# A block of small state matmuls moved by two visits in a fused Mamba-2 scan and feed-forward kernel

## The chip, the cores and the metric

The kernel runs on one core of a Trainium2 chip. Its time is the device time of one execution in microseconds. Three runs of the kernel before the change took 364.34, 364.67 and 365.81 us; their median, 364.67, is the time before. One more execution was profiled, and all durations below are from that one.

## The reference

Two blocks are computed one after the other, in float32. The first is a Mamba-2 scan over x of shape (4, 8, 768, 32) with 16 states per head. It can be evaluated in chunks. Within a chunk:

```
cum     = cumsum(log a)                      # along the chunk
y_intra = ((C B^T) * exp(cum_i - cum_j) * causal) x
y_inter = (C state) * exp(cum)               # what the state before gives
y       = y_intra + y_inter
state   = exp(sum log a) * state + sum_j exp(cum_end - cum_j) B_j x_j
```

Its output, reshaped to 3072 tokens of width 256, goes through the second block:

```
h = y @ w_in          # 256 -> 2048
g = h * cos(h)
out = g @ w_out       # 2048 -> 256
```

The feed-forward block holds nearly all the arithmetic.

## The kernel before

**Chunks and visits.** The kernel takes the 768 positions in chunks of 128 (`NC` = 6, numbered 0 to 5), and each chunk in two units of 64. A pass over chunk c runs the feed-forward block for that chunk in 16 visits (`NF` = 16). Visit n = 16 c + f computes 128 columns of h for one half of the chunk's tokens and the other, a bank of 128 × 512 numbers. While the pass over chunk c runs, the scan for chunk c + 1 is prepared piece by piece in its visits. Where the text says "visit 13" it means f = 13 of a pass.

**One visit.** On TensorE `first(n)` (L650) writes hp(n), the 128 × 512 slice of h, into a PSUM bank. Then a chain over two engines makes g: ScalarE rounds h / 2π to a whole number (`wind_k`, L667), VectorE subtracts it (`wind_w`, L673), ScalarE takes the cosine (`gate`, L682), VectorE multiplies it with hp (`gated`, L687). Last, GpSimd makes three sums of slices of the result, gd (`differ`, L712, L714 and L715), for a second product that takes seven multiplications in place of eight (`seven`, L836). TensorE's `second(n - 2)`, two visits later (`LAG` = 2), uses g and gd.

**Visits with seven products in the first matmul, too.** In visits 10 to 12 of the passes over chunks 2, 3 and 4, and in most of the pass over chunk 5 (`runs`, `sevens`), hp is also made with seven products (`first7`, L760 on TensorE). There VectorE and ScalarE add the parts together (L767 to L781) before hp is whole, and the rest of that visit's chain (`wind`, `gate`, `gated`) is issued one visit late, out of the list `late`.

**PSUM.** There are eight banks: two with the tag "h" for hp, two with "o" for the results of the second product, and two pairs with the tag "scan" (`pair`). A seven-product run takes both pairs at its start, one for a share of hp (`at_["hp"]`, its second, fifth, ... visit) and one for parts (`at_["m"]`). So in visits 10 to 14 of the passes over chunks 2, 3 and 4 the banks "h" go to visits 10, 12, 13 and 14 in turn, and visit 11 has a bank of a pair. In the pass over chunk 1 every visit uses the two banks "h" in turn.

**The scan of the next chunk.** In the pass over chunk c (1 to 4), for chunk c + 1: `inner2` (L603) makes C Bᵀ on TensorE; `weights` multiplies it with the decays on VectorE into m; `turn2` makes rT, C with its decay; `add_state` brings the states up to date on VectorE. Then come the two functions that make y in two pair buffers:

- `open2` (L611): 32 products of states with rT (L617), which open the sums of y, and, but for the last chunk, 32 products of x with weighed B through `sums` (L477), which make the sums for the coming states. In the trace each product is two records, so 64 + 64. They work on tiles of 32 × 64 and 64 × 32.
- `finish2` (L623): 64 products of x with m (L629), which close y, on tiles of 64 × 32. Its `take` then copies y on ScalarE into yT (L636), first for one half, then for the other, and the state sums into a new state tile (L489).

y, not complete before finish2, is the input of `first` from the next pass on.

**What sets the order.** It is written out by hand. Each engine executes its instructions in the order of the program and waits at semaphores for the others. Near the end of a pass the order on TensorE is: first(13), second(11), `open2`, first(14), second(12), first(15), `finish2`, second(13), first(0) of the next pass. On ScalarE in visit 15: `wind_k`, the first half of y (`take_y(0)`), `gate`, the second half with the states (`take_y(1)`). DMAs are issued from the queue of SyncE; none belongs to the two functions.

Of the kernel before, what the change touches and what calls it, by code (L numbers as in the profile page):

```python
# [25 lines left out]
def kernel(  # L26
# [18 lines left out]
    NC = S // P  # L45
    DM, DF = moe_w_in.shape
    KT = DM // P
    NF = DF // P
# [23 lines left out]
    def pair(name):  # L72

        return psum.tile([P, 2, 4 * P], FP32, tag="scan", bufs=2, name=name)
# [52 lines left out]
    def load(c, i):  # L127
        if c < NC:
            for s in range(2):
                (load_x if i in (1, 2) else load_b)(2 * c + i // 2, s)  # L130

    def group(q, s):
        return slice(32 * (q ^ s), 32 * (q ^ s) + 32)
# [477 lines left out]
    def open2(c):  # L611

        ys[c] = y = [pair("y") for _ in range(2)]
        for k, p, s, q in ((k, p, s, q) for k in range(2) for p in range(2) for s in range(2)
                           for q in range(4)):
            r, o_, i = group(q, s), W * (q % 2), (2 * k + p) * W
            PE.matmul(y[s][o_:o_ + W, q // 2, i:i + W], lhsT=after[2 * c + k - 1][r, s, p],  # L617
                      rhs=part[c, s][2][r, p, k * W:(k + 1) * W], start=(k == p == 0), stop=False,
                      tile_position=(r.start, o_), skip_group_check=True)
        for k in range(2 if c < NC - 1 else 0):  # L620
            sums(2 * c + 1 + k, [y[s][:, 0, (2 + k) * P:(3 + k) * P] for s in range(2)], group)

    def finish2(c):  # L623

        y = ys.pop(c)
        for k, p, t, s, q in ((k, p, t, s, q) for k in range(2) for p in range(2)
                              for t in range(2) for s in range(2) for q in range(4)):
            ss, i, h = slice(s * W, (s + 1) * W), (2 * k + p) * W, 4 * t + q
            PE.matmul(y[s][32 * q:32 * q + 32, t, i:i + W], lhsT=xrs[2 * c + k][ss, p, h],  # L629
                      rhs=m_of[2 * c + k][ss, p, h], start=False, stop=True,  # L630
                      tile_position=(s * W, 32 * q), skip_group_check=True)
        yT[c] = two.tile([P, 2, 2, 2 * P], FP32, tag="yT", name="yT")

        def take(k):
            for s in range(2):
                ACT.copy(out=yT[c][:, k, :, s * P:(s + 1) * P], in_=y[s][:, :, k * P:(k + 1) * P])  # L636
            if k and c < NC - 1:
                take_sums((2 * c + 1, 2 * c + 2), [y[s][:, 0, 2 * P:] for s in range(2)])
        return take
# [36 lines left out]
    def wind(n):  # L676
        wind_k(n)
        wind_w(n)

    def gate(n):  # L680
        cos = turns[n]
        ACT.activation(cos, cos, AF.Sin, bias=quarter, scale=TWO_PI)  # L682
# [421 lines left out]
    for n in range(AHEAD, NC * NF + LAG):  # L1104
        c, f = divmod(n, NF)
        if n < NC * NF:

            if c > 0 and f in (loads_of := (6, 7, 8, 9) if c == 1 else (0, 1, 2, 3)):
                load(c + 2, loads_of.index(f))
            if n in (NF - 4, NF - 3):  # L1110
                load_arow(n - NF + 8)
            if n == NF - 2:
                for k in (4, 5):
                    for s in range(2):
                        load_x(k, s)
            if n in (NF - 1, NF):
                load_along(2, (2 * (n == NF), 2 * (n == NF) + 1))
            for e, i in chunks_at(n, "along"):
                load_along(e + 1, (2 * i, 2 * i + 1))
            if n in sevens or n - 1 in sevens:  # L1120
                first_of_seven(n)
            else:
                first(n)
            if n not in sevens and n - 1 in sevens:
                wind(n - 1)
                gate(n - 1)
                gated(late.pop())
            closing = f == NF - 1 and 1 <= c < NC - 1
            take_y = finish2(c + 1) if closing else None
            if n not in sevens:  # L1130
                wind_k(n)
                wind_w(n)
            if closing:
                take_y(0)
            for e, s in chunks_at(n - 1, "turn"):
                turn2(e, s)
            for k in units_at(n, 2):
                turn_unit(k)
            if n + 1 in piece:
                rests_of.append(grade(*piece[n + 1], later=True))  # L1140
            if n not in sevens:
                gate(n)
            while len(rests_of) > (n == AHEAD):
                rest = rests_of.pop(0)
                if rest:
                    rest()
            joins = n in piece and piece[n] in held
            if joins:
                join(*piece[n])

            behind = [lambda at=at: decays2(*at) for at in decays_at(n)]
            behind += [lambda k=2 * c - 1 + i: add_state(k) for c, i in chunks_at(n, "state")]
            behind += [lambda c=c, b=2 * s + p: reaches(c, b) for c, s in chunks_at(n, "reach")
                       for p in range(2)]
            behind += [lambda at=at: turn_blocks(*at) for at in chunks_at(n, "turn")]
            behind += [lambda k=k, p=p: decays0(k, p) for k, at in unit_at.items()
                       for p in range(2) if at[0][p] == n]
            behind = [lambda k=2 * c + i, q=q: weights(k, q) for c, i in chunks_at(n, "weigh")
                      for q in range(2)] + behind
            behind = [lambda k=k: weights(k, 1) for k in units_at(n - 1, 3)] + behind  # L1160
            if not joins and behind:
                behind.pop(0)()
            if n + 1 in sevens or n in sevens:
                late.append(n)
            else:
                gated(n)
            if closing:
                take_y(1)
            if n == NF + 7:
                weigh0(5)  # L1170
            if add_s and (n == NF - 5 or units_at(n - 1, 4)):
                exchange = add_s()
                add_s = None
            if n == NF + 9:
                exchange()
            for do in behind:
                do()
            if n == runs[-1][0] - 2:
                for i in range(4):
                    differ_y(NC - 1, i, V)  # L1180
            if 2 <= c < NC - 1 and 4 <= f <= 7:
                differ_y(c, f - 4, G, slice(1, 2))
            if unsummed and (n in sevens or summed[0]):
                unsummed[0](range(summed[0], summed[0] + 1), G)
                summed[0] = (summed[0] + 1) % 4
                if summed[0] == 0:
                    unsummed.pop()
            elif n not in sevens and f not in ((10, 11, 12) if c == 1 else (10, 11)):
                for do in unsummed:
                    do()  # L1190
                unsummed.clear()
            for k, ((_, last_), *_) in unit_at.items():
                if last_ == n:
                    weigh0(k)
        for i, js in differ_at.get(n, ()):
            differ_w(i, js)
        for start, js in zip((2 * NF - 5, 3 * NF - 3, 4 * NF - 3),
                             (slice(2, 5), slice(0, 2), slice(5, NJ))):
            if start <= n < start + 4:
                differ_in(n - start, js)  # L1200
        if n == AHEAD + 1:
            second(AHEAD - LAG)
        if n >= LAG and n != AHEAD:
            second(n - LAG)
        for e, _ in chunks_at(n, "inner"):
            inner2(e)
        for k in units_at(n, 3):
            for t in range(2):
                inner(k, t)
            if k == 3:  # L1210
                at = [gs[k, s][:, 0, 2 * P:] for s in range(2)]
                sums(4, at, group)
                take_sums((4,), at)
            weights(k, 0)
        for k in units_at(n, 4):
            take_s, add_s = finish0(k)
            take_s()
        for k in units_at(n, 1):
            reach_unit(k)
        if f == NF - 3 and 1 <= c < NC - 1:  # L1220
            open2(c + 1)
        for at, e in block_loads.items():
            if at == n:
                loading = load_blocks(e)
            if at <= n < at + 12:
                next(loading)
# [30 lines left out]
```

## Time and profile before

| What | us |
|---|---|
| Runs: lowest, median, highest | 364.34, 364.67, 365.81 |
| Profiled execution, first to last instruction (the span) | 369.8 |
| TensorE, matmuls: busy | 359.4 (97%) |
| VectorE: busy | 270.8 (73%) |
| GpSimd: busy | 233.0 (63%) |
| ScalarE: busy | 182.3 (49%) |

The page gives the profiled execution's span and no other time of its own; it is 5.1 us longer than the median of the timed runs. The row of the granted clock shows full speed but for one slice of the forty, after a wait of 4.2 us on TensorE in the pass over chunk 1.

How to read it: a row of a timeline has the start, the time it took, the engine, the line of the kernel, the operation, what it writes from what it reads, the tile, and how many records are merged in the row. In brackets stands how long the engine had been idle before it and what it then had waited for. TensorE's records overlap at their ends, so a distance between two starts tells more than a length. PE is TensorE, PEld its weight loads, DVE VectorE, ACT ScalarE, POOL GpSimd, SP SyncE.

### The profile page before, as it was taken

The numbers are of one execution on the slowest core, as the hardware profiler recorded it, in microseconds if no ns is written. First come the engines' busy times: TensorE is split into PE (matmuls) and PEld (weight loads), VectorE is DVE, ScalarE is ACT, GpSimd is POOL, SyncE is SP. The second block draws the span as 40 slices with busy tenths as digits, with TensorE's granted clock in tenths as the row PEclk, the third lists the DMA queues.
The fourth block names the chain that finished last, engine by engine and source line by source line (L and its number), as shares of the span: only waits on it lengthen the run. The fifth ranks groups of instructions, "written<-read, shape, count | busy, mean of one in ns | idle before, by whom it ended". The sixth has DMA issues, their size and how long they took to land.

```text
span 369.8 us, 10169 instructions
## 1 busy us (share of the span) xinstructions
PE 359.4 (97%) x4034; PEld 327.8 (89%) x4034; DVE 270.8 (73%) x492; ACT 182.3 (49%) x346; POOL 233.0 (63%) x375
## 2 busy tenths in 40 slices
PE   8999999999959999999999999999999999999995
PEld 5688888898948989999999999999999999999995
DVE  7699988588735794887757788756796565688874
ACT  4588756463433435453545453445553444455542
POOL 6567656679816676466676656679556465375572
PEclk9999999999996999999999999999999999999999
DMA  7996855593566416344005441001010001001002
GB/s 141 259 361 133 186 119 92 82 151 64 125 100 90 88 44 98 52 79 82 13 4 110 59 79 37 6 4 42 2 30 0 2 2 31 2 2 29 2 10 51
DMA packets 97328, 26.43 MB, mean 71 GB/s; under 512 B 87328, under 2 KB 93184, under 8 KB 97280
## 3 DMA queue, kind: packets, MB, share of 16 engines
q1 hardware_dynamic: 96032, 25.38, 33.7%
q8 instruction: 32, 0.52, 0.6%
q10 hardware_dynamic: 1248, 0.39, 0.5%
q14 instruction: 16, 0.13, 0.1%
HBM read 22.36 MB, written 3.34 MB: 69 GB/s over the span
## 4 chain that ended last, share of the span: by engine, by line
PE 83%; DVE 4%; POOL 3%; ACT 2%; DMA 2%; SPq 2%; issue 2%; DVEq 0%; ACTq 0%; POOLq 0%
PE o L836 31%; PE hp L660 30%; PE m L760 5%; PE o L796 5%; PE hp L760 4%; PE y L629 2%; PE g L603 1%; DMA blocks<-in_C_dram 1%; SPq L150 1%; POOL gd L712 1%; DVE mag L261 1%; DMA bc<-in_B_dram 1%; POOL gd L714 1%; DVE w L673 1%; PE y L617 1%
## 5 line engine op out<-in xcount | busy, mean ns | idle before, releaser
L660 PE MATMUL hp<-yT,w_in 128*128 128x256 f32 x592 | 143.0, 386 | 0.4 <-DVE gT L687 0.4
L660 PEld LDWEIGHTS hp<-yT,w_in 128*128 128x128 f32 x592 | 108.8, 192 | 15.6 <-issue 1.6
L712 POOL TENSOR_TENSOR gd<-gT 128x256 f32<-128x256 f32 x79 | 59.8, 758 | 89.4 <-DVE gT L687 74.3
L682 ACT ACTIVATE w<-w,quarter 128x512 f32<-128x512 f32 x96 | 69.4, 723 | 68.1 <-DVE w L673 68.0
L673 DVE SCALAR_TENSOR_TENSOR w<-hp,k 128x512 f32<-128x512 f32 x96 | 65.8, 685 | 50.3 <-ACT k L667 50.0
L667 ACT ACTIVATE k<-hp 128x512 int32<-128x512 f32 x96 | 57.1, 595 | 77.8 <-PE hp L660 70.4
L687 DVE TENSOR_TENSOR gT<-hp,w 128x512 f32<-128x512 f32 x96 | 65.5, 682 | 17.2 <-ACT w L682 12.5
L836 PE MATMUL o<-words,gd 128*128 128x128 f32 x474 | 66.1, 276 | 0.1
L836 PEld LDWEIGHTS o<-words,gd 128*128 128x128 f32 x474 | 59.4, 192 | 0.3 <-POOL gd L714 0.3
L836 PE MATMUL o<-w_out,gT 128*128 128x128 f32 x316 | 50.1, 278 | 0.0
L836 PEld LDWEIGHTS o<-w_out,gT 128*128 128x128 f32 x316 | 46.6, 193 | 3.2
L714 POOL TENSOR_TENSOR gd<-gT,gd 128x128 f32<-128x128 f32 x79 | 40.4, 512 | 6.2
L715 POOL TENSOR_TENSOR gd<-gT,gd 128x128 f32<-128x128 f32 x79 | 39.0, 494 | 6.2
L836 PE MATMUL o<-w_out,gd 128*128 128x128 f32 x158 | 30.7, 276 | 0.0
L836 PE MATMUL o<-words,gT 128*128 128x128 f32 x158 | 30.6, 275 | 0.0
L796 PE MATMUL o<-w_out,gT 128*128 128x256 f32 x128 | 29.9, 379 | 0.0
L375 DVE TENSOR_TENSOR_SCAN lam<-arow,unit 128x512 f32<-128x512 f32 x20 | 29.8, 1489 | 0.0
L796 PEld LDWEIGHTS o<-w_out,gT 128*128 128x128 f32 x128 | 24.3, 190 | 3.2
L836 PEld LDWEIGHTS o<-words,gT 128*128 128x128 f32 x158 | 24.0, 192 | 0.0
L836 PEld LDWEIGHTS o<-w_out,gd 128*128 128x128 f32 x158 | 24.0, 192 | 0.0
L760 PE MATMUL m<-m,wid 128*128 128x128 f32 x132 | 18.3, 275 | 0.0
L760 PE MATMUL hp<-yT,w_in 128*128 128x128 f32 x88 | 17.0, 275 | 0.0
(130 smaller groups left out, 429.9 us busy)
## 6 DMA issues: line engine op xcount, KB each, us to landing
words<-in_moe_w_in_dram SPq DMA_DIRECT2D x8, 512.0 KB
words<-in_moe_w_out_dram SPq DMA_DIRECT2D x8, 512.0 KB
xr<-in_x_dram SPq DMA_DIRECT2D x24, 128.0 KB
arow<-a_cut SPq DMA_DIRECT2D x10, 256.0 KB
arow<-a_cut SPq DMA_DIRECT2D x10, 252.0 KB
out_dram<-sum SPq DMA_DIRECT2D x18, 128.0 KB
bc<-in_B_dram SPq DMA_DIRECT2D x24, 64.0 KB
blocks<-in_B_dram SPq DMA_DIRECT2D x16, 32.0 KB
```

Source lines behind the costliest of these rows:

```text
L375: V.tensor_tensor_scan(out=lams[k][:, p, hs].rearrange(flat), data0=rows_.rearrange(flat), data1=unit0[:, hs].rearrange(flat), initial=0.0 ...
L660: PE.matmul(to_[:, e], lhsT=w_in[:, k, fs], rhs=y[:, k], start=(k == 0), stop=(k == KT - 1), skip_group_check=True)
L667: ACT.activation(k, hp[n], AF.Copy, bias=0.25, scale=INV_2PI)
L673: V.scalar_tensor_tensor(out=w, in0=hp[n], scalar=INV_2PI, in1=k, op0=ALU.mult, op1=ALU.subtract)
L682: ACT.activation(cos, cos, AF.Sin, bias=quarter, scale=TWO_PI)
L687: V.tensor_tensor(out=gT[n], in0=hp.pop(n), in1=cos, op=ALU.mult)
L712: G.tensor_tensor(out=d[:, 0:2], in0=g[:, 1:2].to_broadcast([P, 2, P]), in1=g[:, 3::-3], op=ALU.subtract)
L714: G.tensor_tensor(out=d[:, 2], in0=g[:, 0], in1=d[:, 0], op=ALU.subtract)
L715: G.tensor_tensor(out=d[:, 3], in0=g[:, 2], in1=d[:, 2], op=ALU.subtract)
L760: PE.matmul(dst[q], lhsT=w[q], rhs=y_[q], start=(q in (6, 1, 7)), stop=True, skip_group_check=True)
L796: PE.matmul(o[c, u][:, t], lhsT=g[:, 2 * e + t], rhs=w_out[:, 2 * j + e], start=(j == e == t == 0), stop=(j == NJ - 1 and e == 1), skip_gr ...
L836: PE.matmul(at[q], lhsT=a_[q], rhs=w[q], start=(j == 0 and q in starts), stop=(j == NJ - 1), skip_group_check=True)
```

## The change

`open2(c + 1)` is called in visit 15 instead of visit 13: directly ahead of `finish2(c + 1)`, after first(15), where it stood at the end of visit 13, after second(11). This holds in the passes over chunks 1, 2, 3 and 4. Nothing else is changed.

```
@@ -1126,6 +1126,8 @@
                 gate(n - 1)
                 gated(late.pop())
             closing = f == NF - 1 and 1 <= c < NC - 1
+            if closing:
+                open2(c + 1)
             take_y = finish2(c + 1) if closing else None
             if n not in sevens:
                 wind_k(n)
@@ -1217,8 +1219,6 @@
             take_s()
         for k in units_at(n, 1):
             reach_unit(k)
-        if f == NF - 3 and 1 <= c < NC - 1:
-            open2(c + 1)
         for at, e in block_loads.items():
             if at == n:
                 loading = load_blocks(e)
```

The order on TensorE becomes: first(13), second(11), first(14), second(12), first(15), `open2`, `finish2`, second(13), first(0).

## The prediction

> **What bounds the kernel now.** I read the page first: which engine is full, at which clock, and who makes the chain that ended last.
>
> ```profile
> PE 359.4 (97%) x4034; PEld 327.8 (89%) x4034; DVE 270.8 (73%) x492; ACT 182.3 (49%) x346; POOL 233.0 (63%) x375
> PEclk9999999999996999999999999999999999999999
> PE 83%; DVE 4%; POOL 3%; ACT 2%; DMA 2%; SPq 2%; issue 2%; DVEq 0%; ACTq 0%; POOLq 0%
> ```
>
> TensorE bounds it: 97% busy, 83% of the chain. An edit that leaves the number of matmuls alone can only matter through TensorE's waits and gaps. So the second view is who TensorE waits for (total us, times, longest):
>
> ```profile
> PE g L603 <- ACT cT L591: 4.2, 1, 4.2
> ...
> PE hp L660 <- DVE gT L687: 0.4, 1, 0.4
> ```
>
> The 4.2 is one late load in chunk 1 (105.6 to 110.8 us), before any moved instruction. None of the waits lies in the visits that the change touches (13 to 15 of the passes over chunks 1 to 4). There TensorE is never late, and the question is whether it stays so. The third view is TensorE in order of time around the moved block; this is the pass over chunk 2, which prepares chunk 3 (start, length, both us):
>
> ```profile
> 186.88 0.61 PE L836 MATMUL o<-w_out,gT 128*128 128x128 f32 x4
> ...
> 188.21 0.39 PE L836 MATMUL o<-w_out,gd 128*128 128x128 f32 x2
> 188.53 0.91 PE L617 MATMUL y<-rT,state 32*64 32x64 f32 x64
> 189.37 0.86 PE L477 MATMUL y<-xr,sc 64*32 64x64 f32 x64
> 190.16 1.99 PE L660 MATMUL hp<-yT,w_in 128*128 128x256 f32 x8
> 191.99 0.61 PE L836 MATMUL o<-w_out,gT 128*128 128x128 f32 x4
> ...
> 193.55 1.89 PE L660 MATMUL hp<-yT,w_in 128*128 128x256 f32 x8
> 195.38 1.48 PE L629 MATMUL y<-m,xr 64*32 64x64 f32 x128
> 196.79 0.71 PE L836 MATMUL o<-w_out,gT 128*128 128x128 f32 x4
> ```
>
> Read it as visits: second(11) from 186.88, the moved block (L617, L477) from 188.53 to 190.16, first(14), second(12), first(15), finish2 (L629) and second(13). Starts follow each other without a hole. A plain first takes 1.73 (193.55 to 195.38 is 1.83, with 0.10 of entry into finish2, see below), a plain second 1.56, the block 1.63, finish2 1.41.
>
> **What the block hides now.** first(14) writes the PSUM bank of hp(12): tag "h" has two banks, visits 12, 13 and 14 take turns on them (visit 11 has its own). That bank is free when gated(12) on VectorE (L687) has read it. The chain to it, ScalarE first, then VectorE with the same row in the other two passes and one old stall:
>
> ```profile
> 186.16 0.60 ACT L667 ACTIVATE k<-hp 128x512 int32<-128x512 f32 x1 [1.09 <-DVE hp L781]
> 187.51 0.72 ACT L682 ACTIVATE w<-w,quarter 128x512 f32<-128x512 f32 x1 [0.76 <-DVE w L673]
> ```
>
> ```profile
> 33.19 0.68 DVE L687 TENSOR_TENSOR gT<-hp,w 128x512 f32<-128x512 f32 x1
> ...
> 185.78 0.29 DVE L781 TENSOR_TENSOR hp<-hp,m 128x128 f32<-128x128 f32 x1
> 186.79 0.69 DVE L673 SCALAR_TENSOR_TENSOR w<-hp,k 128x512 f32<-128x512 f32 x1 [0.72 <-ACT k L667]
> 188.34 0.69 DVE L687 TENSOR_TENSOR gT<-hp,w 128x512 f32<-128x512 f32 x1 [0.86 <-ACT w L682]
> ...
> 245.59 0.69 DVE L687 TENSOR_TENSOR gT<-hp,w 128x512 f32<-128x512 f32 x1 [0.86 <-ACT w L682]
> ...
> 302.24 0.69 DVE L687 TENSOR_TENSOR gT<-hp,w 128x512 f32<-128x512 f32 x1 [0.86 <-ACT w L682]
> ```
>
> hp(12) comes from a seven-product visit, so its last piece is a VectorE addition (L781, 185.78); then k, w, cosine and product follow one another, each waiting for the one before, and the bank is free at 188.34 + 0.69 = 189.03. Without the block, first(14) would start at 188.21 + 0.22 (the spacing of such pairs) = 188.43. So the block, 1.63 long, covers a VectorE chain that is 0.6 late. This chain depends on nothing that moves.
>
> **The change, part by part.**
>
> *Removed from visit 13.* The 128 matmul records of the block (64 in the last pass, which has no state sums) go from behind second(11): TensorE reaches first(14) earlier by 1.63 plus the change of tile shape. No other engine and no queue has an instruction in the block; it issues no DMA.
>
> *The new wait at first(14).* The price of such a wait is in the trace once: the product at 33.19 ends at 33.87, and TensorE's first starts at 34.01, 0.14 later, and then takes 1.81 where 1.73 is plain, 0.08 more. Pass over chunk 2: 189.03 + 0.14 − 188.43 = 0.74. Chunk 3: 245.59 + 0.69 + 0.14 − 245.43 = 0.99 (the last pair of second(11) starts at 245.13 and is 0.07 long over its usual 0.39). Chunk 4: 302.24 + 0.69 + 0.14 − (302.13 + 0.22) = 0.72. In the pass over chunk 1 there are no sevens, and gT(12) starts at 129.78 and ends at 130.46 while first(14) could start at 131.38: no wait, 0.8 of room. Sum of waits 2.45, restarts 3 × 0.08 = 0.24. Bounds: if the 0.14 and 0.08 do not count, 2.03; if the wait costs also what the page shows for VectorE products held up once by GpSimd (0.34 ahead of the product at 242.43), in all three passes, 2.7 + 1.0 = 3.7. I take 2.69, from the row that is the same wait.
>
> *What is behind it.* Queued behind first(14) on TensorE are second(12), first(15), the block, finish2. ScalarE's k(14) waits for first(14); it still comes about 0.9 us earlier than before. second(12) needs gd(12): GpSimd ran it from 189.17 to 190.98; second(12) would start at 189.17 + 1.81 = 190.98, and its first use of a difference is its third product, 0.45 later, of the part that is ready at 190.44. Room 0.9. first(15) needs gT(13), ended 191.17, and starts at 192.54. In the pass over chunk 1 GpSimd ends the first difference that is used at 132.78 and second(12) would want it at 133.11 + 0.45: room 0.8.
>
> *Added to visit 15.* The block runs between first(15) and finish2, 1.63 as before. Its operands are old by then (state additions in visits 0 and 5, and 12 for chunk 2; weighed B in visit 11 or earlier), and the two pair banks have been free since visit 13. Behind it: ScalarE's take_y(0) waits for finish2 and the cosine of visit 15 is queued behind take_y(0), VectorE's gated(15) behind that. But second(13), which covers take_y(0) (1.56 against two copies of 0.65 together), follows finish2 as before, so from the end of finish2 on everything stands as it did. Price nothing; if that cover were gone, first(16) would wait up to 0.65 a pass. sc, rT and states buffers come free two visits later and are next written in visit 4 or later of the next pass, except sc, which has three buffers and whose next writer (visit 15) takes an older one: nothing.
>
> *Changes of tile shape.* From 128×128 products into the block there is a gap of 0.10 (188.43 to 188.53), out of it first(14) takes 1.83 instead of 1.73; the same around finish2 (195.28 to 195.38; the four products from 196.79 take 0.55 to the next start, where 0.44 is plain). Side by side the two share one entry and one exit: −0.20 a pass, 4 passes, −0.8. L477 and L629 have the same tile (64 × 32), so no new change comes between them in passes 1 to 3. Bounds: 0 (the gaps belong to something else) and −0.8.
> The Trainium skill, "TensorEngine Tiling (Array Packing)", Tiling Modes, says that changing the tiling mode drains the engine while another tile of the same mode does not. The last pass has no L477 between L617 (32 × 64) and L629 (64 × 32), so by that rule one drain stays there and the gain is −0.7; by the trace, which shows L617 to L477 (the same two shapes) at 0.84 with no visible hole, −0.8.
>
> *Sum:* 2.69 − 0.8 = +1.9. The page gives the profiled execution a span of 369.8, 5.1 over the median of the timed runs (364.67); it holds the 4.2 us wait and a stretch at half clock after it, which the timed runs need not have. Both lie ahead of the change, so I add the difference to the median: 366.6 (+0.5%). Own range, from the bounds: 2.03 − 0.8 = +1.2 to 3.7 − 0.8 = +2.9, so 365.9 to 367.6.
>
> **Rivals.**
>
> *No wait (not slower).* If first(14) does not stall, because the bank is free sooner than the recorded end of the product, only the shared changes of shape are left: −0.8, 363.9. For it: all three waits are under 1 us, and one rotation of banks read wrongly undoes them. Against: the wait of 33.19 is the same pair of instructions. It decides where the three waits sum to less than 0.8.
>
> *A second wait behind the first.* GpSimd's three operations for gd(12) are the next thing late. Their longest records are 1.65, 1.42 and 1.33 where VectorE runs a scan beside them. With the first two so long, the part for second(12) is ready at 189.17 + 1.65 + 0.08 + 1.42 = 192.3 against 191.4: 0.9 more a pass, 2.7 in three, 369.3. Against: in visits 12 and 13 VectorE has no scan.
>
> *The clock falls.* After the 4.2 us wait the granted clock was 0.5 for 6.8 us and a first took 3.58. If each new wait did that, 3 × 3.4 (half of 6.8) = 10 more, 376.8. Against: after the 0.35 us of idle time ahead of 34.01 the clock stayed full, and 0.7 to 1.0 is much nearer to that.
> The Trainium skill, "TensorE: Matmul & The Clock Gate", Part 1, has the clock halved after an idle window of about 3.4 us; by it these waits cost no clock and the sum stays 366.6, while by the 4.2 us row alone it could be 376.8.
>
> **How the numbers follow.** Forecast 62%, no wait 15%, second wait 18%, clock 3%, something else 2%. What a measurement of this kernel can tell from no change is about 0.5%, 1.8 us, and the forecast lies at that bound: I split it 55 to 45 between slower and same. Slower: 0.34 + 0.18 + 0.03 = 0.55. Same: 0.28 + 0.10 of the no-wait case = 0.38. Faster: the rest, 0.07. Range: down to the no-wait case with the spread of the runs, 363.6; up into the second wait, 368.8.
>
> **What would show it.** Right: TensorE's list of waits gains L660 waiting for gT L687, three times, 0.7 to 1.0 each, in visit 14 of the passes over chunks 2, 3 and 4 and none in that over chunk 1; L617, L477 and L629 stand together without a gap; second(13) follows at once. Wrong: no such wait, gaps inside the joined block, a wait of L836 for gd, or a second 6 in the clock row.

## The result, and the profile after

The changed kernel takes 377.21 us in the median of six runs (375.69 to 380.04), against 364.76 for the kernel before (six runs, 364.34 to 365.81): a ratio of 1.0348, 95% interval 1.0314 to 1.0382. The prediction said 366.6, with a range up to 368.8. It had the sign; of the 12.5 us that the change cost it had 1.9.

The page of the profiled execution (380.04 us), the rows that answer to those shown of before:

```profile
span 378.2 us, 10169 instructions
PE 360.3 (95%) x4034; PEld 329.1 (87%) x4034; DVE 270.3 (71%) x492; ACT 182.1 (48%) x346; POOL 234.2 (62%) x375
PEclk9899999999999999999998999998999999999999
PE 77%; DVE 6%; SPq 5%; issue 4%; ACT 3%; POOL 3%; DMA 2%; DVEq 0%; ACTq 0%; POOLq 0%
```

The same 4034 matmul records, 2 points less busy, and two slices below full clock in the second half of the run, where there were none (a third lies in the opening). Whom TensorE waits for (total us, times, longest):

```profile
PE y L629 <- issue: 6.3, 3, 2.2
...
PE hp L660 <- DVE gT L687: 2.3, 4, 0.8
```

The second row is the forecast: three new waits of first(14), beside the old one of 0.35. The first row was not foreseen. TensorE stood still three times for about 2 us inside finish2, and "issue" means that it waited for nothing that the profile shows. TensorE in order of time, the passes over chunks 1, 2, 3 and 4:

```profile
137.69 1.02 PE L629 MATMUL y<-m,xr 64*32 64x64 f32 x79 [1.96 <-issue]
...
187.96 1.96 PE L660 MATMUL hp<-yT,w_in 128*128 128x256 f32 x8 [0.58 <-DVE gT L687]
189.76 0.61 PE L836 MATMUL o<-w_out,gT 128*128 128x128 f32 x4
...
191.32 1.89 PE L660 MATMUL hp<-yT,w_in 128*128 128x256 f32 x8
193.15 0.91 PE L617 MATMUL y<-rT,state 32*64 32x64 f32 x64
193.99 0.80 PE L477 MATMUL y<-xr,sc 64*32 64x64 f32 x60
...
194.65 1.42 PE L629 MATMUL y<-m,xr 64*32 64x64 f32 x117
198.27 0.44 PE L629 MATMUL y<-m,xr 64*32 64x64 f32 x9 [2.21 <-issue]
198.65 1.22 PE L836 MATMUL o<-w_out,gT 128*128 128x128 f32 x4
...
201.71 1.89 PE L660 MATMUL hp<-yT,w_in 128*128 128x256 f32 x8
...
259.40 1.08 PE L629 MATMUL y<-m,xr 64*32 64x64 f32 x66 [2.11 <-issue]
...
316.14 0.91 PE L617 MATMUL y<-rT,state 32*64 32x64 f32 x64
316.98 1.24 PE L629 MATMUL y<-m,xr 64*32 64x64 f32 x104
```

The joined run starts at 193.15 and flows without a hole from L617 over L477 into L629, as forecast. Then, with 9 of its matmuls to go, it stops for 2.21 us. In the pass over chunk 1 it stops with 79 to go, in that over chunk 3 with 66, in that over chunk 4 not at all; there, with no sums for coming states, the joined run is 384 records long and not 512 (the last row above holds 104 of finish2's 128 matmuls because its window ended at 318 us). Behind the second gap second(13) takes 3.06 (198.65 to 201.71): the clock is at half for 3.4 us. It was so behind two of the three gaps here. Before the change second(13) took 1.66, from 196.79 in the prediction's rows to the row that follows them:

```profile
198.45 1.89 PE L660 MATMUL hp<-yT,w_in 128*128 128x256 f32 x8
```

**Where the gaps stand.** Counting TensorE's records in the trace (weight loads, matmuls and waits, in order of start), the three gaps come at records 3009, 4545 and 5825. All three leave 193 when divided by 256 (why 193 and not 0, the trace doesn't show). The page has a DMA queue for instructions with 32 packets and 0.52 MB, so 16 KB each:

```profile
q8 instruction: 32, 0.52, 0.6%
```

TensorE's 8168 records fill 32 packets of 256. In the kernels with 9064 and 9960 records, further down, the queue has 35 and 39 packets, which is the number of blocks of 256 from record 193 on; so the queue is TensorE's. Beside the packets of this queue the block ends read like this (worked out from the trace, us):

```
pass, kernel      a block end reached   packet on q8        next block end    between
chunk 1, after    2753 at 133.98        135.41 to 136.41    3009 at 137.69    3.71, gap
chunk 2, after    4289 at 194.51        195.96 to 196.88    4545 at 198.27    3.76, gap
chunk 3, after    5569 at 255.54        256.98 to 257.91    5825 at 259.40    3.86, gap
chunk 4, after    6849 at 316.16        314.09 to 315.13    7105 at 317.65    1.49
chunk 2, before   4289 at 193.44        193.20 to 194.46    4545 at 196.53    3.09
```

In the three passes with a gap, the packet sets out 1.4 us after a block end is reached, takes 1.0, and TensorE goes on 1.3 to 1.5 later: 3.7 to 3.9 in all, while a run of short records uses 256 in 1.5. These packets are no slower than the other two in the table. Which block a packet carries the trace doesn't say; they are paired by time. Nor do they always set out behind a block end: in the pass over chunk 4 the packet left 2.1 us ahead of it, and in slow stretches of both kernels up to 2.6 us ahead.

### The profile page after: what moved, and what is told of

It reads as the page before. It is cut to its first block, busy times and chain, and to the rows that moved or that the text cites. A ratio compares the mean times of both kernels' runs of the same rounds, so it can differ in the third digit from the quotient of the medians.

```text
span 378.2 us, 10169 instructions
## 1 busy us (share of the span) xinstructions
PE 360.3 (95%) x4034; PEld 329.1 (87%) x4034; DVE 270.3 (71%) x492; ACT 182.1 (48%) x346; POOL 234.2 (62%) x375
## 4 chain that ended last, share of the span: by engine, by line
PE 77%; DVE 6%; SPq 5%; issue 4%; ACT 3%; POOL 3%; DMA 2%; DVEq 0%; ACTq 0%; POOLq 0%
PE o L836 30%; PE hp L660 27%; PE m L760 5%; PE hp L760 3%; PE o L796 3%; DMA bc<-in_C_dram 2%; PE y L629 2%; DVE gT L687 2%; DVE w L673 2%; PE g L603 1%; SPq L147 1%; PE g L456 1%; SPq L165 1%; PE y L477 1%; ACT k L667 1%
## 5 line engine op out<-in xcount | busy, mean ns | idle before, releaser
L660 PE MATMUL hp<-yT,w_in 128*128 128x256 f32 x592 | 140.9, 382 | 2.3 <-DVE gT L687 2.3
L836 PE MATMUL o<-words,gd 128*128 128x128 f32 x474 | 67.4, 280 | 0.1
L836 PEld LDWEIGHTS o<-words,gd 128*128 128x128 f32 x474 | 60.7, 196 | 0.3 <-POOL gd L714 0.3
L836 PE MATMUL o<-w_out,gT 128*128 128x128 f32 x316 | 50.8, 281 | 0.0
L836 PEld LDWEIGHTS o<-w_out,gT 128*128 128x128 f32 x316 | 46.9, 195 | 3.2 <-issue 0.3
L714 POOL TENSOR_TENSOR gd<-gT,gd 128x128 f32<-128x128 f32 x79 | 41.5, 525 | 6.2
L715 POOL TENSOR_TENSOR gd<-gT,gd 128x128 f32<-128x128 f32 x79 | 40.7, 515 | 6.2
L836 PE MATMUL o<-words,gT 128*128 128x128 f32 x158 | 31.0, 279 | 0.0
L836 PE MATMUL o<-w_out,gd 128*128 128x128 f32 x158 | 30.9, 277 | 0.0
L375 DVE TENSOR_TENSOR_SCAN lam<-arow,unit 128x512 f32<-128x512 f32 x20 | 28.8, 1441 | 0.0
L836 PEld LDWEIGHTS o<-words,gT 128*128 128x128 f32 x158 | 24.5, 196 | 0.0
L836 PEld LDWEIGHTS o<-w_out,gd 128*128 128x128 f32 x158 | 24.3, 194 | 0.0
L465 DVE TENSOR_TENSOR m<-g,lam 128x512 f32<-128x512 f32 x24 | 16.2, 682 | 1.3 <-PE g L456 1.0
```

Source lines behind the costliest of these rows:

```text
L375: V.tensor_tensor_scan(out=lams[k][:, p, hs].rearrange(flat), data0=rows_.rearrange(flat), data1=unit0[:, hs].rearrange(flat), initial=0.0 ...
L660: PE.matmul(to_[:, e], lhsT=w_in[:, k, fs], rhs=y[:, k], start=(k == 0), stop=(k == KT - 1), skip_group_check=True)
L714: G.tensor_tensor(out=d[:, 2], in0=g[:, 0], in1=d[:, 0], op=ALU.subtract)
L715: G.tensor_tensor(out=d[:, 3], in0=g[:, 2], in1=d[:, 2], op=ALU.subtract)
L836: PE.matmul(at[q], lhsT=a_[q], rhs=w[q], start=(j == 0 and q in starts), stop=(j == NJ - 1), skip_group_check=True)
```

## The experiments

**The theories.** A, instruction supply: TensorE's records come in blocks of 256; the next block but one can be asked for only when a block end is reached, and takes about 3.75 us; an unbroken run of short records that is much longer than 256 uses up what is there and waits. open2 and finish2 are 256 records each (loads and matmuls; open2 is 128 in the pass over chunk 4), the joined run 512. (That a block can be asked for "only" at a block end is too narrow, by the packets that left ahead of one.) B, adjacency: finish2 adds to the PSUM banks that open2 has just written, and is held until they have settled. C, the place: an operand or a bank of the block is late in its new place.

**One slow group between the two.** open2 goes to the end of visit 14, so that first(15) lies between it and finish2.

```
-        if f == NF - 3 and 1 <= c < NC - 1:
+        if f == NF - 2 and 1 <= c < NC - 1:
             open2(c + 1)
```

> open2 stands at the end of visit 14, between second(12) and first(15): one slow product group lies between it and finish2. Theory A (instruction supply: TensorE's records arrive in blocks of 256, 16 KB each, a block comes about 3.75 us after it can be asked for, and an unbroken run of short records uses 256 in 1.6 us): no run is longer than 256 records, so no gap that waits for nothing; what remains are the three waits of first(14) for the product of visit 12, 0.7 to 1.0 us each, and the clock stays full: 364.8 + 2.1 to 2.7 = 367.2. Theory B (adjacency: finish2 adds to the PSUM banks that open2 has just written and is held until those results have settled): no gap either, same time. Theory C (the block's operands or banks come late at its new place): a gap of about 2 us ahead of or inside the block remains.

Measured: 368.41, ratio 1.0119 (1.0084 to 1.0154), 1.2 us above the 367.2 expected. TensorE's waits:

```profile
PE hp L660 <- DVE gT L687: 2.3, 4, 0.8
PE y L515 <- issue: 2.0, 1, 2.0
```

No gap in finish2 or in the block. L515 is in the opening of the kernel, from 15.7 us on. The three waits of first(14) stand as in the changed kernel. Taking the ends of finish2, the passes over chunks 2, 3 and 4 are 0.93, 1.20 and 0.80 longer than before, 2.93 in all. In the first two, 0.12 of that is finish2 itself, which takes 1.53 and not 1.41. Up to the start of finish2 it is 0.82, 1.08 and 0.80: 2.70 for the waits, where the prediction had 2.69. The block with all its operands is not late one visit earlier; for visit 15 that says little, so C is left to the next runs. A and B both stand.

**The block twice, finish2 apart.** The kernel before the change, with open2's products issued twice in visit 13 (`sums` keeps its operand for the second copy).

```
+        for again in range(2):
             for k, p, s, q in (...):
                 ...
             for k in range(2 if c < NC - 1 else 0):
                 sums(...)
```

> As before the change, but the block of open2 is issued twice in visit 13 (the second copy starts its sums again, so the result is the same); finish2 stays apart. Theory A: a run of 512 short records in the passes over chunks 1, 2 and 3, so one gap of about 2.1 us in each, at a record number that leaves 193 when divided by 256, and none in the pass over chunk 4 (256 records): 364.8 + 5.7 of extra work + 6.3 + 0 to 5 of lowered clock = 377 to 382. Theory B: no finish2 in the run, so no gap: 370.5. Theory C: no gap: 370.5.

Measured: 375.02. The pass over chunk 1 (in this kernel the lines behind 616 are one higher):

```profile
126.18 1.20 PE L618 MATMUL y<-rT,state 32*64 32x64 f32 x64
127.30 0.34 PE L477 MATMUL y<-xr,sc 64*32 64x64 f32 x16
128.93 0.72 PE L477 MATMUL y<-xr,sc 64*32 64x64 f32 x48 [1.29 <-issue]
```

The gap is there with finish2 out of reach, in the passes over chunks 1, 2 and 3, at records 3009, 4545 and 6337, 193 modulo 256 each time, and in that over chunk 4 none. C had no gap here either. B as stated falls. The second copy does write banks that the first has just written, so a wider B is not out by this run alone; but the gaps lie 416, 301 and 442 records into runs of 512 that are alike, and the next runs keep the order and move the gap. The size was off: 1.3 to 1.4 us and not 2.1. From block end to block end it is 3.44, 3.21 and 3.23 here, at the low end of what later runs gave (3.2 to 4.0). The clock stayed full, so the total lies at 375.02 and under the 377 to 382 expected.

**Half of the move.** L617 stays in visit 13, the sums (L477) go in front of finish2: a run of 384.

```
+            if closing:
+                open_sums(c + 1)     # the sums, taken out of open2
             take_y = finish2(c + 1) if closing else None
```

> Half of the move: the state products (L617) stay in visit 13, only the sums for states (L477) go to visit 15 ahead of finish2. The run is 384 records in the passes over chunks 1 to 3. Theory A: the run starts at records 2783, 4178 and 5573 of TensorE's stream; block ends (193 modulo 256) lie 226, 111 and 252 records into it, so only in the second run does a whole further block end inside it (record 367 of 384): a gap of about 2.1 us in the pass over chunk 2 and none in the other two. L617 alone (0.84) still covers first(14)'s wait, but for 0.1 in the pass over chunk 3. 364.8 + 2.2 + 0 to 1.7 of lowered clock = 367.0 to 368.7. Theory B: the sums and finish2 write the same banks side by side in all three passes: three gaps, 371 to 376; or none, if only L617's banks count: 364.8. Theory C: sums late in visit 15: three gaps.

Measured: 367.61, ratio 1.0095 (1.0067 to 1.0122). The pass over chunk 1 has no gap, that over chunk 2 has one (finish2's line is 633 here):

```profile
130.75 1.65 PE L633 MATMUL y<-m,xr 64*32 64x64 f32 x126
132.34 0.71 PE L840 MATMUL o<-w_out,gT 128*128 128x128 f32 x4
...
187.72 1.55 PE L633 MATMUL y<-m,xr 64*32 64x64 f32 x117
191.46 0.32 PE L633 MATMUL y<-m,xr 64*32 64x64 f32 x9 [2.19 <-issue]
```

One gap, at record 4545, in the pass that was named, at the place that was named, in an order of work that is the same in all three passes. This is what A alone says; B and C have no reason to pick one pass of three.

**The same order, every record 120 numbers later.** 30 tiny products are issued by TensorE at the very start (`ones128` and `ones8` stand for constants).

```
+    pad = bank([P, 2, P], "warm", "o")
+    for _ in range(30):
+        PE.matmul(pad[:, 0, 0:8], lhsT=ones128, rhs=ones8, start=True, stop=True)
```

> The kernel of the run that moved only the sums, with 30 tiny products (120 records) issued by TensorE at the very start, where it waits for loads: the order of the work is the same, only every later record has a number 120 higher. Theory A: block ends now lie 106, 247 and 132 records into the runs of 384 in the passes over chunks 1, 2 and 3: the gap of the pass over chunk 2 goes, and gaps of 1.5 to 2.4 us appear in the passes over chunks 1 and 3 (in the latter a block end comes just behind the run), all at 193 modulo 256. Theories B and C: the gap stays where it was, in the pass over chunk 2, because the order around it is unchanged.

```profile
146.70 0.33 PE L633 MATMUL y<-m,xr 64*32 64x64 f32 x11 [1.91 <-issue]
...
203.96 1.62 PE L633 MATMUL y<-m,xr 64*32 64x64 f32 x126
205.51 0.71 PE L840 MATMUL o<-w_out,gT 128*128 128x128 f32 x4
...
262.59 0.49 PE L840 MATMUL o<-w_out,gT 128*128 128x128 f32 x2
264.76 0.49 PE L840 MATMUL o<-w_out,gT 128*128 128x128 f32 x2 [1.69 <-issue]
```

The gap of the pass over chunk 2 is gone; gaps stand in the passes over chunks 1 and 3, at records 3265 and 6081, the second just behind the run in second(13), as expected. Nothing in the scan or the feed-forward part had been touched: only the number of each record. The total, 382.30, can't be compared, since the padding alone took about 9.5 us at the start and two more gaps came in the opening.

**Three copies.** As the run with two, with 768 records.

> The block of open2 three times in visit 13, a run of 768 records (384 in the pass over chunk 4). Theory A: two gaps of 1.3 to 2.4 us in each of the passes over chunks 1 to 3, 256 records apart, the time from one block end to the second next being 3.2 to 4.0 us in a run however often it is repeated; 375.0 + 5.7 of further work + 3 to 4 further gaps of 1.8 = 386 to 392 with the clock's part. Theory B: one gap at most, 381.

Measured: 394.95. Two gaps in each of the passes over chunks 1 to 3, 256 records apart, and one in the pass over chunk 4. The pass over chunk 1:

```profile
128.73 0.72 PE L477 MATMUL y<-xr,sc 64*32 64x64 f32 x48 [1.32 <-issue]
129.39 1.11 PE L618 MATMUL y<-rT,state 32*64 32x64 f32 x64
130.42 0.47 PE L477 MATMUL y<-xr,sc 64*32 64x64 f32 x16
132.19 0.97 PE L477 MATMUL y<-xr,sc 64*32 64x64 f32 x48 [1.30 <-issue]
```

3.46 us for the second 256 records, of which 1.3 is standing still: the supply sets the pace, and the price is per block and not once per run. The total lies 3 us over the upper end; in three passes the clock was at half for 6.8 us each, more than that sum had room for.

**The wait taken away.** In the changed kernel first(14) writes the unused second bank of the pair of visit 11 (`at_["two"]`).

```
+            elif n - 2 in sevens and c < NC - 1:
+                first(n, to_=at_["two"][:, 1])     # the pair that holds visit 11's share
             else:
                 first(n)
```

> The changed kernel, but first(14) of the passes over chunks 2, 3 and 4 writes the unused second bank of the pair that visit 11 uses, so it need not wait for the product of visit 12. All theories: the three waits of 0.6 to 0.9 us go, the issue gaps inside the block stay at about 2.1 us: 377.2 - 2.1 to 2.5 = 375, if the block doesn't then wait for the product of visit 14, which holds that pair (at most 0.5 a pass).

Measured: 375.80, ratio 1.0298 (1.0232 to 1.0364). The waits of first(14) are gone and open2 waits 0.2 once for the product of visit 14, which holds the pair. But a fourth gap has come, in the pass over chunk 4:

```profile
PE y L629 <- issue: 7.7, 4, 2.1
...
PE y L617 <- DVE gT L687: 0.2, 1, 0.2
```

So the time fell by 1.4 and not by 2.1 to 2.5, a difference that lies within the spread of either kernel's runs (375.69 to 380.04, and 372.23 to 377.62). In the changed kernel the block end of that pass (record 6849) lies 9 records into the run, and its packet had set out 2 us before TensorE got there. Here the packet set out 0.8 us after. A wait ahead of the run may have kept TensorE from asking early; that was not tried by itself.

**Both kernels once more, profiled.**

> The kernel before, profiled once more. Theory A: no gap in the passes over chunks 1 to 4 (no run over 256 records); the 4.2 us wait for a late load and the half clock after it, which the first profile had, need not come again: a span near 362.9, the timed median less 1.8. Without them the opening shows what it takes in an ordinary execution.

> The changed kernel, profiled once more. Theory A: the three gaps stand at the same records again (3009, 4545 and 5825, 193 modulo 256), 1.9 to 2.4 us each, and none in the pass over chunk 4; what differs from execution to execution is how many of them halve the clock for 3.4 us (two in the first profile), about 1.7 us each: 374 to 380.

Before: 364.35. The late load of the first profile did not come again, the clock is full throughout, and there is no gap in the passes. After: 378.19, with the gaps at the same three records, and this time the clock fell behind all three.

```profile
PE y L629 <- issue: 6.8, 3, 2.4
PE hp L660 <- DVE gT L687: 2.3, 4, 0.8
```

These two profiles can be laid side by side, matmul by matmul. The changed kernel is 0.7 us late ahead of the first moved block, and then 4.0, 8.6, 13.2 and 13.8 behind the passes over chunks 1 to 4. The passes so cost 3.3, 4.5, 4.6 and 0.6, together 13.1. By terms: gaps 6.8; waits 2.7, as measured by themselves with the block in visit 14; second(13) at half clock 2.93, 2.91 and 2.76 where 1.66 is usual, 3.6 more; shared changes of tile shape −0.8. The sum is 12.3. It closes in the passes over chunks 1 and 4; the 0.8 that is missing lies in those over chunks 2 and 3. Part of it is the rest of finish2, which ran at half clock too: in the pass over chunk 3 its last 66 matmuls took 1.16, where 79 took 0.95 at full clock (pass over chunk 1 of the first profile).

**Shifting the kernel before.** Two kernels with padding ahead of the work of before were to show that its runs of 256 are safe wherever block ends lie, and perhaps to save the gap in the opening.

> The kernel before the change, with 20 tiny products (80 records) ahead at TensorE's start, so that block ends move by 80 records. Theory A: no run is longer than 256 records, so no gap in the passes over chunks 1 to 4, wherever the block ends lie; the gap at record 449 in the opening (0.3 us in the profile of before, up to 2 in other executions) moves or goes: 364.7 with a difference of -1.0 to +0.7. Theories B and C say nothing of it: 364.7.

> The kernel before with 40 tiny products on a 32 x 32 tile (160 records of some 11 to 13 ns) ahead at TensorE's start, where it waits for loads, so that block ends of the opening lie at records in which it waits anyway. Theory A: the gap at record 449 (0.3 to 2 us) goes and none comes in the passes: 364.7 - 1.0 to + 0.5. If the opening is bound by its loads and not by the gap: no difference.

The first part held, but for 0.2 us at record 2241 (193 modulo 256, too) in the first of them: neither has a further gap in the passes over chunks 1 to 4, with records shifted by 80 and by 160. The times did not: 376.87, ratio 1.0312 (1.0286 to 1.0337), and 369.19, ratio 1.0101 (1.0052 to 1.0150). The padding took some 8 and 4 us of the opening, where I had taken it for free, and gaps of 2.6 us at record 449, now in other work, and of 1.8 us at record 705 stood in the opening. So the supply costs time in the opening as well, and no version came out ahead of the kernel before.

## Why the prediction was wrong

- *The new wait at first(14): right.* Three waits, in the passes over chunks 2, 3 and 4, none in the pass over chunk 1; 2.69 forecast with the restarts, 2.70 measured by themselves, and pass by pass 0.82, 1.07 and 0.80 against 0.82, 1.08 and 0.80.
- *What is behind it: right.* No wait of L836 for gd appeared, and first(15) did not wait. The rivals "no wait" and "a second wait" are out.
- *Changes of tile shape: not contradicted.* The run flows from L617 over L477 into L629 without a hole. In the pass over chunk 4, where only the wait and the shapes change, the cost was 0.6, against 0.80 for the wait alone with the block in visit 14: −0.2, as forecast. If a drain stays there between L617 and L629, as the rule that the prediction cites has it, it did not cost the 0.1 that the prediction would have given it: L617 takes 0.84 to the start of L629, as it took to that of L477. In the other passes the gaps hide this term.
- *Added to visit 15: wrong, and this is the step that failed.* "The block runs between first(15) and finish2, 1.63 as before" and "price nothing" put the joined run at the sum of its parts. The trace of before held no run of more than 256 records in these passes, so it had no price for one of 512, and I set no bound on it. The price was a wait for instructions in three of the four passes, 6.3 to 6.8 us in all. With the waits at 2.7 and the changes of shape at −0.8, the 1.9 forecast, 11.2 of the 13.1 us between the two later profiles are left for the joined run: the gaps and the half clock behind them. The row of q8 stood on the page before, at a share of 0.6%; the prediction has no term for it.
- *The clock falls: dismissed at 3%, and it happened, but not for the waits that I priced.* The waits of 0.6 to 0.8 us left the clock alone, as the row of 0.35 had suggested. The gaps of about 2 us did not: two or three of the three gaps were followed by half clock, at 1.1 to 1.4 us each in second(13) alone. That this rival's total, 376.8, lies within 0.5 us of the 377.21 measured is luck: none of the three stretches of half clock that it adds came where it put them.

The Trainium skill, "Runtime: NRT & Kernel Launch", Instruction fetch mechanics, would have pointed at the mechanism: it has the instructions refilled in blocks of 16 KiB, 256 of them, with which the traces agree, 16 KB a packet and gaps 256 records apart. It also calls the crossing of a block mostly hidden and gives TensorE room for 2048 instructions. In these runs a crossing cost up to 2.4 us, and a run of 384 was enough for one.

## What to carry to other kernels

Before two groups of short instructions are put side by side, count their records. On TensorE, in the passes of these kernels, 512 in a row met a gap of 1.3 to 2.4 us in twelve runs of twelve, 384 in or just behind five runs of ten, depending on where the block ends lay, and 256 in none. A full engine that waits for "issue" at places a fixed number of records apart is short of instructions by these runs, and shifting every record by a constant tells it from a dependency. A slow group between two short ones is not only an interruption; as first(15) did with the block in visit 14, it can give the next block time to come.

## What the runs showed of the hardware that I had not expected

- From one block end to the end of a block that was not there in time took 3.2 to 4.0 us on TensorE in the passes, 23 gaps in seven profiles of six kernels; 256 short records need 1.5 to 1.6.
- The place of a gap is fixed by the record's number: 193 modulo 256 in every gap for instructions of every profile, in the opening as well (record 449 in several, 0.3 to 2.6 us).
- The clock went by periods of 3.41 us: every stretch of half clock that the profiles record and that ended inside a kernel lasted 3.41, 6.83 or 10.24 us, and all stretches of one profile begin on one grid of 3.41. In the passes, a period in which TensorE stood still for 1.9 us or more (seven in the kernels with a gap, at 1.91 to 2.25) was followed by one at half clock; 1.7 or less was not, except in the kernel with three copies, where 1.3 to 1.7 was enough in three passes, while 1.6 in the fourth was not. What made those three different is open: the rest of each was filled with products on small tiles, but so was the period of the half move with 1.6 us of standing still, and full clock followed that. Whether a gap costs this extra time depends on how it falls into the periods, which fits the spread of the changed kernel's runs (375.69 to 380.04). The Trainium skill, "TensorE: Matmul & The Clock Gate", Part 1, asks for a whole idle window of about 3.4 us; here some 56% of one was enough.
